# Reordering the front of a fused cross-attention and maxout kernel: state casts, state transposes, the first state read, and idle matmuls at the end

## The chip, the cores and the metric

The kernel runs on one core of a Trainium2 chip. The metric is the device time of one execution in microseconds (us), lower is better. Before the change five runs gave 149.58, 149.90, 149.92, 150.22 and 150.27 us, so the median is 149.92 us.

The engines are named as in the profile: PE is TensorE, DVE is VectorE, ACT is ScalarE, POOL is GpSimd, and SP is the engine whose queue issues nearly all DMA transfers here. PEld is the loading of weights into TensorE.

## What is computed

Eight batches, eight heads, 512 tokens `x` and 32 states `state` of width 64 per head. Tokens read the states and states read the tokens, and the concatenation of both goes through a layer that takes the larger of two products:

```python
scores = scale * x @ state.T            # 512 x 32 for each head
xread  = softmax(scores) @ state        # 512 x 64
scores2 = scale * state @ x.T
sread  = softmax(scores2) @ x           # 32 x 64
t = concat([xread, sread])              # 544 tokens of 8 * 64 = 512
out = maximum(t @ w1, t @ w2) @ w_out   # 512 -> 1024 -> 512
```

Inputs and output are float32; the products run in bfloat16.

## The kernel before

**The algebra.** The maximum is written as relu(t (w1 - w2)) + t w2, so the output is relu(t (w1 - w2)) w_out + t (w2 w_out). `wcat` (128 x 4 x 1536) holds w1 - w2 in its first 1024 columns (`w_sub`, four quarters of 256 columns) and w2 w_out in its last 512 (`w_t` transposes w2, `w_wo` multiplies, `w_wo_out` copies). For each batch the states are multiplied into it once: `u_sw(b, ch)` (L280) makes SW[b] = states x `wcat`, in three chunks `ch` of 512 columns, two of which are for the relu part and the last for the direct one. The attention weights, transposed (`AT[b]`, tile aT), are then multiplied with SW[b] directly, so that xread itself is never formed.

**One batch.** `u_exp` (L216, L219) forms the scores from the transposed tokens `xt` and the block-diagonal states `sbd`, and takes their exponentials `e` on ACT; `u_norm` (L223 to L226) sums, inverts and scales them to `a`; `u_at` or `d_at` transposes `a` into aT; `u_sr` (L239 to L244) makes the state read from `e` and the tokens `xp`, and `u_srt` (L263) transposes it into `sread_t`. `l1` (L308) makes the eight blocks f = 0 to 7 of the hidden layer, each followed by a relu into `r` on ACT and DVE in turn (L296, L298). `l2` has four token groups c: `l2_open` (L319) starts an accumulator with the direct part, `l2_add` (L323) adds `r` times `wo`, `l2_close` copies it out. The state reads of all batches go through the same layer in `moe_sread` near the end.

**PSUM.** Two pools of four banks each turn round: "ps" for everything short, "acc" for the accumulators. A new user of a bank waits until the bank's last reader has finished.

**Where the order comes from.** The schedule is manual: each engine runs its instructions in the order in which the program writes them (L441 to L542). SP likewise issues its transfers in written order, and they share the 16 DMA engines. The order of the loads (L103 to L113) is: states of batch 0, x(0) in two halves, w2 and w_out in pieces, the first 512 columns of w1 in two parts, the second 512 columns of w1, x(1), the states of batches 1 and 2 (`second`), x(2). The rest of the states (`rest`) and x(3) follow later from SP.

**The front, L441 to L530.** It holds, in this order: idle products on a zero tile (`warm_up`, L131); the states of batch 0; tokens of batch 0, cast into `xp` (L180) and transposed on TensorE (L198) into `xt`; scores; w2 cast and transposed while w_out's quarters are cast to `wo` on POOL and multiplied; the first state read; then `u_sw(0, 0)` and `u_sw(0, 2)`, the first half of `l1(0)`, the opens and first adds of `l2(0)` with the states of batches 1 and 2 transposed amid them (L504, L155), `u_sw(0, 1)`, the second half of `l1(0)`, and the preparation of batch 1 between the last adds of batch 0. For batches 1 and 2 the tokens are also cast to a compact copy `xc` (L186), which a DMA transpose (L190) turns into `xt`. From L531 a regular loop takes batches 1 to 7, in which `fillers` puts the next batch's preparation between the products.

Of the kernel before, what the change touches and what calls it, by code (L numbers as in the profile page):

```python
# [15 lines left out]
def kernel(  # L16
# [42 lines left out]
    def copy(eng, o, i):  # L59
        if eng == "A":  # L60
            nc.scalar.copy(o, i)  # L61
        elif eng == "V":
            nc.vector.tensor_copy(o, i)  # L63
        else:
            nc.gpsimd.tensor_copy(o, i)  # L65
# [11 lines left out]
    def load_x(b, parts=1):  # L77
        xf_t[b] = xio.tile([128, H, NC * D], F32, tag="xf", name="xf")
        for g in range(parts):
            nc.sync.dma_start(out=xf_t[b][:, g::parts, :], in_=x[b, g::parts].rearrange("h (p c) d -> p h (c d)", c=NC))  # L80
# [3 lines left out]
    def load_states(bs):  # L84
        nc.sync.dma_start(out=s_f[:, 2 * bs.start:2 * bs.stop],
                          in_=state[bs].rearrange("b (q h) n d -> (h n) (b q) d", q=2))
# [6 lines left out]
    def load_w(t, w, ch, parts=1):  # L93
        cs = slice(ch * 512, (ch + 1) * 512)
        for k in range(parts):
            i = slice(4 * k // parts, 4 * (k + 1) // parts)
            nc.sync.dma_start(out=t[:, i, cs], in_=w.rearrange("(i p) f -> p i f", p=128)[:, i, cs])  # L97
# [9 lines left out]
        load_wo(2 * ch)  # L107
        load_wo(2 * ch + 1)
    load_w(w1f, moe_w1, 0, 2)
    load_w(w1f, moe_w1, 1)  # L110
    load_x(1)
    load_states(second)
    load_x(2)  # L113

    ident = consts.tile([128, 128], BF16)
# [12 lines left out]
    def warm_up(n):  # L128
        p = bank()
        for k in range(n):  # L130
            nc.tensor.matmul(p, warm[:, 0:128], warm, start=(k == 0), stop=(k == n - 1))  # L131


    s_bf = stage.tile([128, 2 * B, 2, D], BF16)
# [25 lines left out]
    def negate_states():  # L160
        for g in range(2):
            gs = slice(64 * g, 64 * g + 64)
            negate("V", sneg[gs], sbd[gs, 0, g::2, g, :])
# [11 lines left out]
    def cast_x(b, parts=(("P", slice(0, 8)),)):  # L175
        new_x(b)
        xp = st[b]["xp"] = xio.tile([128, H, NC, 66], BF16, tag="xp", name="xp")
        nc.gpsimd.memset(xp[:, :, :, 64:65], 1.0)
        for e, hs in parts:
            copy(e, xp[:, hs, :, 0:64], xf_t[b][:, hs].rearrange("p h (c d) -> p h c d", c=NC))  # L180

    def compact_x(b, g, eng="A"):
        new_x(b)
        if g == 0:
            st[b]["xc"] = at.tile([128, H, NC * D], BF16, tag="xc", name="xc")
        copy(eng, st[b]["xc"][:, 4 * g:4 * g + 4], xf_t[b][:, 4 * g:4 * g + 4])  # L186


    def d_xt(b):
# [2 lines left out]
    def u_xt(b, g, eng):  # L192
        d = st[b]
        p = bank(BF16)
        for i in range(4):
            for c in range(NC):
                k = 2 * i + c // 2
                nc.tensor.transpose(p[64 * (c % 2):64 * (c % 2) + 64, k * 128:(k + 1) * 128], d["xp"][:, 2 * i + g, c, 0:64], ident)  # L198
        copy(eng, d["xt"].rearrange("p (i g u) t -> p g i (u t)", g=2, u=2)[:, g], p.rearrange("p (i w) -> p i w", i=4))

    def u_sc(b, g, mul=nc.gpsimd):
# [28 lines left out]
    def u_sr(b):  # L230

        d = st[b]
        d["sr"] = at.tile([128, 2, D], BF16, tag="sr", name="sr")
        d["rr"] = at.tile([128, 2], F32, tag="rr", name="rr")
        p = bank()
        for g in range(2):
            for c in range(NC):
                for i in range(4):
                    nc.tensor.matmul(p[32 * i:32 * i + 32, g * 65:g * 65 + 65], d["e"][:, g, i, c, :],  # L239
                                     d["xp"][:, 2 * i + g, c, 0:65],  # L240
                                     start=(c == 0 and g == 0), stop=(c == NC - 1 and g == 1))
# [146 lines left out]
    def w_cast(o, w, ch, engs="VA"):  # L388
        cs = slice(ch * 512, (ch + 1) * 512)
        for k in range(2):  # L390
            copy(engs[k], o[:, 2 * k:2 * k + 2, cs], w[:, 2 * k:2 * k + 2, cs])
# [26 lines left out]
    def fillers(b):  # L418
        fill = {}

        def put(slot, *units):
            fill.setdefault(slot, []).extend(units)

        n = b + 1
        if n < B:
            put(7, lambda: u_sc(n, 0), lambda: u_sc(n, 1))
            put(8, lambda: u_sr(n))
        if n + 1 < B:
            put(8, lambda: compact_x(n + 1, 0), lambda: compact_x(n + 1, 1))
        if n < B:  # L430
            put(9, lambda: d_at(n))
            put(10, lambda: u_sw(n, 0, 1, 2))
        if n + 1 < B:
            put(10, lambda: d_xt(n + 1))
        if n < B:
            put(11, lambda: u_srt(n))
        return fill

    for b in range(B):
        SW[b] = swt[:, b % 2]  # L440
    warm_up(6)  # L441
    cast_states("V", first)
    states(first)
    warm_up(9)
    cast_x(0, (("A", slice(0, 4, 2)), ("V", slice(4, 8, 2)), ("P", slice(1, 4, 2)), ("V", slice(5, 8, 2))))
    u_xt(0, 0, "V")
    warm_up(2)
    u_xt(0, 1, "A")
    u_exp(0, 0)
    warm_up(2)  # L450
    u_exp(0, 1)
    warm_up(3)
    w_cast(w2b, w2f, 0, "PA")
    u_norm(0, 0, nc.vector)
    u_norm(0, 1, nc.vector)
    w_t(0, 0, "A")
    w_t(0, 1, "A")
    u_sr(0)
    wo_cast(0, "P")
    wo_cast(1, "P")  # L460
    warm_up(1)
    for i in range(4):
        w_wo(0, i)
    u_at(0, "V")
    w_cast(w2b, w2f, 1)
    for i in range(4):
        w_wo(1, i)
    w_t(1, 0, "V")
    w_t(1, 1, "A")
    negate_states()  # L470
    wo_cast(2, "P")
    wo_cast(3, "P")
    u_srt(0)
    warm_up(2)
    for i in range(4):
        w_wo(2, i)
    for e, i in (("P", slice(0, 1)), ("A", slice(1, 2)), ("V", slice(2, 3)), ("A", slice(3, 4))):
# [5 lines left out]
    u_sw(0, 0)  # L483
    u_sw(0, 2)
    w_sub(0)
    w_sub(1)
    l1(0, {}, range(0, 4))
    w_sub(2, nc.vector)
    w_sub(3, nc.vector)
    compact_x(1, 0)  # L490
    compact_x(1, 1)
    d_xt(1)
    load_states(rest)
    cast_x(1, (("A", slice(0, 4)), ("A", slice(4, 8))))
    cast_states("P", second)
    compact_x(2, 0, "P")
    compact_x(2, 1, "P")
    d_xt(2)
    load_x(3)
    for c in range(NC):  # L500
        l2_open(0, c)
    l2_add(0, 0, range(0, 4))
    l2_add(0, 1, range(0, 4))
    states(second)  # L504
    l2_add(0, 2, range(0, 4))
    u_sw(0, 1)
    l2_add(0, 3, range(0, 4))
    l1(0, {}, range(4, 8))
    u_sw(1, 0)
    u_exp(1, 0)  # L510
    u_exp(1, 1)
    u_norm(1, 0, nc.gpsimd)
    u_norm(1, 1, nc.gpsimd)
    cast_states("P", rest)
# [16 lines left out]
    for b in range(1, B):  # L531
        fill = fillers(b)
        if b + 2 < B:
            cast_x(b + 2)
            if b + 3 < B:
                load_x(b + 3)
        if b == 1:
            fill[11].append(lambda: put_states(rest, sT))
        l1(b, fill)
        if b == B - 1:  # L540
            moe_sread()
        l2(b, fill)  # L542


# [28 lines left out]
```

The softmax here doesn't subtract the row's maximum and nothing guards it: scores larger than these inputs give would overflow.

## Time and profile before

| what | value |
|---|---|
| median of the five runs | 149.92 us |
| the profiled execution, its own time | 149.57 us |
| its span, first to last instruction | 147.8 us |
| instructions in it | 3024 |
| PE busy | 141.4 us, 96% |
| DVE, ACT, POOL busy | 81.7, 75.8, 44.2 us |
| granted TensorE clock | 1.000 |
| HBM read and written | 15.20 MB and 8.91 MB |

The page gives each engine's busy time over the whole span and in forty slices. The timeline lists instructions in order of time: start, time taken, engine, line, operation, output and inputs, how many are merged, and in square brackets how long the engine had been idle before and what ended that. The chain of waits goes back from the last instruction through what released each step. PE's busy time includes time in which a product is in the pipe, so neighbouring starts tell more about it than durations do.

### The profile page before, as it was taken

Reading aid. Unit: us, or ns where it says so; the run is one execution under the profiler, and the core shown is the slowest. Engines: PE = TensorE matmul, PEld = TensorE weight load, DVE = VectorE, ACT = ScalarE, POOL = GpSimd, SP = SyncE. Lnnn points to the kernel's source line nnn. Section 1 sums busy time; section 2 is a strip of 40 time slices with the busy share of each in tenths; the row PEclk is TensorE's granted clock in tenths of the full one; section 3 lists DMA queues with packets and bytes.
Section 4 is the critical chain, followed back from the end, with each engine's and each line's share of the span. In section 5 each row is a group of like instructions: output and inputs, shape, how many; then the busy total and the mean of one; then the engine's idle time right before and its main releaser. Section 6 shows DMA issues by size and latency. Waiting matters only on the chain.

```text
span 147.8 us, 3024 instructions
## 1 busy us (share of the span) xinstructions
PE 141.4 (96%) x1249; PEld 67.3 (46%) x1249; DVE 81.7 (55%) x150; ACT 75.8 (51%) x127; POOL 44.2 (30%) x48
## 2 busy tenths in 40 slices
PE   6989899999999999999999999999999999999991
PEld 2445533434454345434443454454445434764460
DVE  5448728758887287545836581667167635721130
ACT  3175548577576268446834691477177036521011
POOL 3145269552957130640072037004100500000000
PEclk9999999999999999999999999999999999999999
DMA  2999999979899969793979497760556031502423
GB/s 72 378 387 386 386 387 342 274 146 218 241 258 330 217 132 304 266 199 125 285 220 174 177 297 175 136 284 2 108 109 284 0 75 64 220 0 71 141 88 133
DMA packets 37982, 29.89 MB, mean 202 GB/s; under 512 B 24912, under 2 KB 33360, under 8 KB 37072
## 3 DMA queue, kind: packets, MB, share of 16 engines
q1 hardware_dynamic: 37824, 29.56, 69.2%
q8 instruction: 10, 0.16, 0.5%
q10 hardware_dynamic: 144, 0.13, 0.3%
q14 instruction: 4, 0.03, 0.1%
HBM read 15.20 MB, written 8.91 MB: 163 GB/s over the span
## 4 chain that ended last, share of the span: by engine, by line
PE 78%; DMA 9%; SPq 9%; POOL 1%; issue 1%; ACT 0%
PE acc L323 35%; PE ps L308 18%; DMA s_f<-in_state_dram 9%; PE acc L319 9%; SPq L97 4%; PE ps L280 3%; SPq L80 3%; PE ps L216 2%; PE ps L367 2%; PE acc L377 2%; SPq L100 2%; PE ps L239 2%; PE acc L357 1%; PE acc L375 1%; PE acc L280 1%; POOL s_bf L65 1%
## 5 line engine op out<-in xcount | busy, mean ns | idle before, releaser
L323 PE MATMUL acc<-wo,r 128*128 128x512 bf16 x248 | 59.0, 379 | 0.0
L323 PEld LDWEIGHTS <-r 128*128 128x128 bf16 x248 | 23.9, 98 | 28.3 <-issue 0.2
L298 DVE TENSOR_SCALAR r<-ps 128x512 bf16<-128x512 f32 x32 | 22.1, 692 | 13.6 <-PE ps L308 13.6
L308 PE MATMUL ps<-aT,swt 128*128 128x512 bf16 x128 | 29.2, 379 | 0.2 <-DVE swt L63 0.2
L226 POOL TENSOR_TENSOR a<-e,er 128x512 bf16<-128x512 bf16 x14 | 14.4, 1048 | 49.1 <-ACT e L219 29.7
L63 DVE COPY ob<-acc 128x512 f32<-128x512 f32 (+1 forms) x17 | 11.1, 655 | 30.2 <-PE acc L323 29.8
L61 ACT COPY ob<-acc 128x512 f32<-128x512 f32 (+1 forms) x16 | 9.2, 574 | 28.8 <-PE acc L323 13.0
L296 ACT ACTIVATE r<-ps 128x512 bf16<-128x512 f32 x32 | 19.3, 602 | 5.7 <-PE ps L308 5.2
L308 PEld LDWEIGHTS <-swt 128*128 128x128 bf16 x128 | 12.0, 98 | 15.0 <-DVE swt L63 0.8
L319 PE MATMUL acc<-swt,aT 128*128 128x512 bf16 x62 | 18.1, 381 | 0.0
L61 ACT CAST swt<-ps 128x512 bf16<-128x512 f32 x18 | 10.0, 589 | 13.0 <-PE ps L280 13.0
L65 POOL CAST xp<-xf 128x2048 bf16<-128x2048 f32 (+1 forms) x7 | 12.2, 1745 | 12.2 <-DMA xf<-in_x_dram 12.2
L61 ACT CAST xc<-xf 128x1024 bf16<-128x1024 f32 x12 | 12.0, 1052 | 1.5 <-DMA xf<-in_x_dram 1.5
L223 DVE TENSOR_REDUCE es<-e 128x16 f32<-128x512 bf16 x16 | 10.6, 660 | 3.6 <-ACT e L219 3.6
L63 DVE CAST swt<-ps 128x512 bf16<-128x512 f32 x18 | 11.6, 679 | 1.1 <-PE ps L280 1.1
L131 PE MATMUL ps<-warm 128*128 128x512 bf16 x25 | 8.0, 447 | 1.3 <-POOL warm L117 1.3
L219 ACT ACTIVATE e<-ps 128x512 bf16<-128x512 f32 x16 | 8.8, 598 | 0.8
L412 PE MATMUL acc<-wo,w2t 128*128 128x512 bf16 x32 | 7.4, 379 | 0.6 <-POOL wo L65 0.6
L319 PEld LDWEIGHTS <-aT 128*128 128x128 bf16 x62 | 4.7, 98 | 6.0 <-issue 2.5
L280 PE MATMUL ps<-wcat,sbd 64*32 64x512 bf16 x136 | 6.2, 383 | 0.1
L216 PEld LDWEIGHTS <-xt 128*128 128x128 bf16 x128 | 4.8, 98 | 2.8 <-ACT xt L61 0.8
L65 POOL CAST wo<-wof 128x1024 bf16<-128x1024 f32 x4 | 4.3, 1064 | 5.1 <-DMA wof<-in_moe_w_out_dram 5.1
(74 smaller groups left out, 119.4 us busy)
## 6 DMA issues: line engine op xcount, KB each, us to landing
xf<-in_x_dram SPq DMA_DIRECT2D x7, 1024.0 KB, 7.6
out_dram<-ob SPq DMA_DIRECT2D x7, 1024.0 KB, 5.0
w2f<-in_moe_w_dram SPq DMA_DIRECT2D x2, 1024.0 KB, 9.0
wof<-in_moe_w_out_dram SPq DMA_DIRECT2D x4, 512.0 KB, 10.9
xf<-in_x_dram SPq DMA_DIRECT2D x2, 512.0 KB, 4.4
w1f<-in_moe_w_dram SPq DMA_DIRECT2D x2, 512.0 KB, 13.3
w1f<-in_moe_w_dram SPq DMA_DIRECT2D x1, 1024.0 KB, 14.1
out_dram<-ob SPq DMA_DIRECT2D x3, 256.0 KB, 2.6
```

Source lines behind the costliest of these rows:

```text
L61: nc.scalar.copy(o, i)
L63: nc.vector.tensor_copy(o, i)
L65: nc.gpsimd.tensor_copy(o, i)
L219: nc.scalar.activation(out=d["e"][:, g].rearrange("p i c n -> p (i c n)"), in_=p, func=ACTF.Exp, scale=scale)
L223: nc.vector.tensor_reduce(d["es"][:, g], d["e"][:, g].rearrange("p i c n -> p (i c) n"), axis=mybir.AxisListType.X, op=ALU.add)
L226: mul.tensor_mul(d["a"][:, g].rearrange("p c i n -> p i c n"), d["e"][:, g], d["er"][:, g].rearrange("p (i c) -> p i c", i=4).unsqueeze(3) ...
L280: nc.tensor.matmul(pg[g][32 * i:32 * i + 32, :], sneg[gs, i, :] if k else sbd[gs, b, 2 * i + g, g, :], w[gs, i, ch * 512:(ch + 1) * 512], ...
L296: nc.scalar.activation(out=o, in_=p, func=ACTF.Relu)
L298: nc.vector.tensor_scalar(o, p, scalar1=0.0, scalar2=None, op0=ALU.max)
L308: nc.tensor.matmul(p, SW[b][:, g, f * 128:(f + 1) * 128], AT[b][:, g, :], start=(g == 0), stop=(g == 1))
L319: nc.tensor.matmul(OB[b][1 + c], AT[b][:, g, c * 128:(c + 1) * 128], SW[b][:, g, FF:WC], start=(g == 0), stop=False)
L323: nc.tensor.matmul(OB[b][1 + c], R[b][:, f, c * 128:(c + 1) * 128], wo[:, f, :], start=False, stop=(f == NF - 1))
```

## The change

In the loads, the second 512 columns of w1 move behind x(1) and the states of batches 1 and 2. At the start six idle products become three, and four later groups go or shrink (two, two, three and one become one; two more go further on). Batch 0's tokens are first cast to the compact `xc`, from which TensorE transposes 128 x 128 blocks, and cast to `xp` later, on ACT. The negated states are made earlier on DVE. The second half of w2's first cast is DVE's instead of ACT's, the second w2 cast goes ahead of aT, and the second w2 transposes stand between the products of w_out's second quarter.

Further on, the state read `u_sr(0)` goes behind the first half of `l1(0)` and its transpose `u_srt(0)` behind the second half. The states of batches 1 and 2 are cast on POOL between the two subtractions `w_sub(0)` and `w_sub(1)`, and transposed between the second and the third open of `l2(0)`. `w_sub(2)` and `w_sub(3)` come later on DVE. The scores of batch 1 move into the second half of `l1(0)`, behind block f = 5. At the very end TensorE gets 26 products of 8 x 8 on the zero tile.

```diff
     load_w(w1f, moe_w1, 0, 2)
-    load_w(w1f, moe_w1, 1)
     load_x(1)
     load_states(second)
+    load_w(w1f, moe_w1, 1)
     load_x(2)
...
+    def pad_stream(n):
+        p = bank()
+        for k in range(n):
+            nc.tensor.matmul(p[0:8, 0:8], warm[:, 0:8], warm[:, 0:8], start=(k == 0), stop=(k == n - 1))
...
-            for c in range(NC):
-                k = 2 * i + c // 2
-                nc.tensor.transpose(p[64 * (c % 2):64 * (c % 2) + 64, k * 128:(k + 1) * 128], d["xp"][:, 2 * i + g, c, 0:64], ident)
+            for cp in range(2):
+                k = 2 * i + cp
+                nc.tensor.transpose(p[:, k * 128:(k + 1) * 128], d["xc"][:, 2 * i + g, cp * 128:(cp + 1) * 128], ident)
...
-    warm_up(6)
+    warm_up(3)
     cast_states("V", first)
     states(first)
     warm_up(9)
-    cast_x(0, (("A", slice(0, 4, 2)), ("V", slice(4, 8, 2)), ("P", slice(1, 4, 2)), ("V", slice(5, 8, 2))))
+    negate_states()
+    compact_x(0, (("A", slice(0, 4, 2)), ("V", slice(4, 8, 2)), ("P", slice(1, 4, 2)), ("V", slice(5, 8, 2))))
     u_xt(0, 0, "V")
-    warm_up(2)
     u_xt(0, 1, "A")
     u_exp(0, 0)
-    warm_up(2)
     u_exp(0, 1)
-    warm_up(3)
-    w_cast(w2b, w2f, 0, "PA")
+    warm_up(1)
+    w_cast(w2b, w2f, 0, "PV")
     u_norm(0, 0, nc.vector)
     u_norm(0, 1, nc.vector)
     w_t(0, 0, "A")
     w_t(0, 1, "A")
-    u_sr(0)
     wo_cast(0, "P")
     wo_cast(1, "P")
-    warm_up(1)
     for i in range(4):
         w_wo(0, i)
+    w_cast(w2b, w2f, 1)
     u_at(0, "V")
-    w_cast(w2b, w2f, 1)
-    for i in range(4):
-        w_wo(1, i)
+    w_wo(1, 0)
+    w_wo(1, 1)
     w_t(1, 0, "V")
     w_t(1, 1, "A")
-    negate_states()
+    w_wo(1, 2)
+    w_wo(1, 3)
+    cast_x(0, (("A", slice(0, 4)),))
+    copy("A", st[0]["xp"][:, 4:8, :, 0:64], xf_t[0][:, 4:8].rearrange("p h (c d) -> p h c d", c=NC))
     wo_cast(2, "P")
     wo_cast(3, "P")
-    u_srt(0)
-    warm_up(2)
...
     w_sub(0)
+    cast_states("P", second)
     w_sub(1)
     l1(0, {}, range(0, 4))
-    w_sub(2, nc.vector)
-    w_sub(3, nc.vector)
-    compact_x(1, 0)
-    compact_x(1, 1)
+    u_sr(0)
+    compact_x(1)
     d_xt(1)
     load_states(rest)
     cast_x(1, (("A", slice(0, 4)), ("A", slice(4, 8))))
-    cast_states("P", second)
-    compact_x(2, 0, "P")
-    compact_x(2, 1, "P")
+    l2_open(0, 0)
+    l2_open(0, 1)
+    states(second)
+    l2_open(0, 2)
+    l2_open(0, 3)
+    w_sub(2, nc.vector)
+    w_sub(3, nc.vector)
+    l2_add(0, 0, range(0, 4))
+    l2_add(0, 1, range(0, 4))
+    compact_x(2, (("P", slice(0, 4)), ("P", slice(4, 8))))
     d_xt(2)
     load_x(3)
-    for c in range(NC):
-        l2_open(0, c)
-    l2_add(0, 0, range(0, 4))
-    l2_add(0, 1, range(0, 4))
-    states(second)
     l2_add(0, 2, range(0, 4))
     u_sw(0, 1)
     l2_add(0, 3, range(0, 4))
-    l1(0, {}, range(4, 8))
     u_sw(1, 0)
-    u_exp(1, 0)
-    u_exp(1, 1)
+    l1(0, {5: [lambda: u_exp(1, 0), lambda: u_exp(1, 1)]}, range(4, 8))
+    u_srt(0)
     u_norm(1, 0, nc.gpsimd)
     u_norm(1, 1, nc.gpsimd)
...
         l2(b, fill)
+    pad_stream(26)
```

`compact_x` now takes a list of engines and head ranges, as `cast_x` did; what it does for batches 1 to 7 stays as it was.

More of the change, by code (lines that the diff above doesn't have):

```diff
@@ L180, in cast_x, with compact_x @@
             copy(e, xp[:, hs, :, 0:64], xf_t[b][:, hs].rearrange("p h (c d) -> p h c d", c=NC))
-    def compact_x(b, g, eng="A"):
+    def compact_x(b, parts=(("A", slice(0, 4)), ("A", slice(4, 8)))):
         new_x(b)
-        if g == 0:
-            st[b]["xc"] = at.tile([128, H, NC * D], BF16, tag="xc", name="xc")
-        copy(eng, st[b]["xc"][:, 4 * g:4 * g + 4], xf_t[b][:, 4 * g:4 * g + 4])
+        xc = st[b]["xc"] = at.tile([128, H, NC * D], BF16, tag="xc", name="xc")
+        for e, hs in parts:
+            copy(e, xc[:, hs], xf_t[b][:, hs])
     def d_xt(b):
@@ L428, in fillers @@
         if n + 1 < B:
-            put(8, lambda: compact_x(n + 1, 0), lambda: compact_x(n + 1, 1))
+            put(8, lambda: compact_x(n + 1))
         if n < B:
```

## The prediction

> **What bounds the kernel now.** I read the page first, by its 40 slices, to see where TensorE waits and for whom.
>
> ```profile
> PE   6989899999999999999999999999999999999991
> ...
> GB/s 72 378 387 386 386 387 342 274 146 218 241 258 330 217 132 304 266 199 125 285 220 174 177 297 175 136 284 2 108 109 284 0 75 64 220 0 71 141 88 133
> ...
> PE 78%; DMA 9%; SPq 9%; POOL 1%; issue 1%; ACT 0%
> ```
>
> One slice is 3.7 us. TensorE has gaps only in the first six; there the transfers run at a level 386 GB/s. From 26 us on TensorE is full. The chain of waits shows the seam:
>
> ```profile
> 14.48 13.45 DMA s_f<-in_state_dram
> 27.93 0.05 issue
> 27.98 1.15 POOL s_bf L65
> 29.14 0.05 issue
> 29.18 0.40 PE ps L155 x4
> ```
>
> After 29.18 it holds TensorE pieces alone up to 144.59. But the states, late as they are, cost little: the previous group, 8 products (L323) from 27.23 at 0.216 each (the steady starts: 16 in 3.45), ends at 28.96, so the wait is 0.22. What starts the full stretch lies earlier. The timeline from 21 to 24.5 us:
>
> ```profile
> 21.48 0.43 DVE L63 CAST w1b<-w1f 128x512 bf16<-128x512 f32 x1 [2.66 <-DMA w1f<-in_moe_w_dram]
> ...
> 21.83 1.28 DVE L63 CAST wcat<-acc 128x512 bf16<-128x512 f32 x2
> ...
> 23.03 1.28 DVE L63 CAST swt<-ps 128x512 bf16<-128x512 f32 x2
> ...
> 23.76 1.04 PE L308 MATMUL ps<-aT,swt 128*128 128x512 bf16 x4 [0.21 <-DVE swt L63]
> ```
>
> VectorE idles 2.66 us for the second half of w1's first 512 columns, then runs four copies, and the first l1 product starts at 23.76. TensorE arrives at the same point by its own road: wo's third quarter lands at 17.5, its cast ends at 18.57, 16 products (L412) fill 18.62 to 22.07. So **the start of l1(0) at 23.76 is set by transfers; from there TensorE sets the time.** l1(1) starts at 39.85, and batches 1 to 7, whose order of instructions is unchanged, follow without a gap. The whole question: does 23.76 move, and does the stretch of 16.09 us from there to 39.85 get longer or shorter?
>
> **Before 23.76: nothing.** Removed are 12 of 25 idle products (0.427 apart at first, 0.216 later), 16 transposes (32 of 64x128, 0.64 per 16, become 16 of 128x128; 0.5 per 8 by the w2b transposes, L401, 16 in 1.06; 0.32 by 0.040 each if width were free), u_sr(0) (0.37) and u_srt(0) (0.06). All of it lies beside transfers: the w2b transposes wait at 10.53 for the POOL cast of w2f, the products at 18.62 for wo. The transfers up to w1's first half keep their place on SP, so 17.5 and 21.43 stand. The ScalarE copies of xp(0), 2 x 1.04, moved behind the w2t copy (ends 18.58), end by 20.7; the first w1b cast slips from 20.13 to 20.7 and ends at 21.3, still ahead of the 21.48 one. The copies hold the x buffer for load_x(2), issued at 20.64 anyway. On VectorE the w2b cast (0.68) goes ahead of the softmax sums (es 9.88 to 10.1); the second w2b cast goes ahead of aT, 14.95 to 15.6; aT is wanted at 23.76. The negation (1.09) fits ahead of x's second half (6.70). Cover gone, these would cost at most their durations, one for one.
>
> The row for the clock: idle products start 0.43 apart up to 3.4 us and the 16 at 18.62 run at 0.216, right behind the longest idle of TensorE, 0.61 us; that gap grows to some 1.1 us (17.5 to 18.6). [...]
>
> **The stretch from 23.76, in the new order** (listed from the changed program; durations from the chain of waits: 2 products 0.43, 8 are 1.73; state-weight products with their hand-over 0.44; scores 0.47; u_sr 0.37).
>
> 25.50 u_sr(0), 25.87 two opens, 26.73 state transposes (0.24), 26.97 two opens, 27.83 three adds, 30.52 u_sw(0,1), 30.86 add, 31.82 u_sw(1,0), 32.16 l1 f4 and f5, 33.02 scores of batch 1, then f6, f7, u_srt(0), add. Who must be ready:
>
> - *States.* Loads issued on SP behind w1's first half were w1's second half, x(1), states, x(2), landing at about 24.3, 27.41, 27.93, 31.04. Now x(1) takes the first place (24.3), the states 24.8 (0.52 behind x(1), as before), and w1's second half, last of the same three, 27.9. SP issues the same list inside 10.19 to 20.46, x(2) still behind. On POOL: subtraction 0 ends at 24.0, cast 1.15 to 26.0, TensorE wants it at 26.73: the wait of 0.22 goes. Subtraction 1 ends at 28.5 (before 26.44); u_sw(1,0) wants it at 31.82.
> - *w1's second half.* VectorE: f3 to 26.39, state-read normalisation 0.46, sbd copies 27.16 to 28.02, subtractions 2 and 3 (2.35) to 30.39, wanted at 30.52. It just fits; before it had 1.7 us to spare (28.66 against 30.38). This is late next: each us of landing after 28.0 is a us lost.
> - *x(1).* ScalarE compacts at 25.87 instead of 27.41, so the DMA transpose is issued at 27.98 instead of 29.43; 4.4 to landing gives 32.4. Scores want it at 33.0. The old wait for xt, 0.11, goes.
> - *Banks.* The old second group of scores waited 0.16 (0.63 against 0.47) for VectorE's f7. Now the first waits about 0.05 for its swt copy (to 33.01).
> - *ScalarE.* Here is the new wait. In these rows of before
>
> ```profile
> 33.13 0.60 ACT L296 ACTIVATE r<-ps 128x512 bf16<-128x512 f32 x1 [0.27 <-PE ps L308]
> ...
> 33.90 0.68 PEld L216 LDWEIGHTS <-xt 128*128 128x128 bf16 x16 [0.33 <-DMA xt<-xc]
> 33.90 0.80 PE L216 MATMUL ps<-sbd,xt 128*128 128x64 bf16 x16
> ...
> 34.44 1.10 ACT L219 ACTIVATE e<-ps 128x512 bf16<-128x512 f32 x2
> ...
> 34.53 1.03 PE L323 MATMUL acc<-wo,r 128*128 128x512 bf16 x4
> ```
>
> f6's relu (33.13) is done before the exponentials, and the adds start at once. In the new order the scores stand between f5 and f6, so f6's relu queues behind two exponentials: scores at 33.07, exponentials 0.54 later, 33.61 to 34.71, relu f6 to 35.31. TensorE has done f6, f7, u_srt by 34.46, adds f4 and f5 by 34.89, and waits for f6 until 35.37: 0.48. Behind it on ScalarE stand sread_t and the swt copies, whose readers come later.
>
> After that: u_sw(1,1) at 35.90 against 35.49. POOL's weights a(1) end at about 38.6 (before 38.26), wanted at 38.8, so nothing more is added and l1(1) starts at 40.26.
>
> **Sum.** Moved in +0.43; waits gone -0.49 (0.22, 0.11, 0.16); new waits +0.53 (0.05, 0.48); shorter hand-overs in my list -0.06: **+0.41 us**.
>
> *The pad.* 26 pairs of 8-column products are not in the trace: 0.029 each by the 64-column scores, 0.06 by the state transposes, so 0.75 to 1.6 us from 144.6. The last copy and store run there until 147.8, 3.2 us: zero; with no cover, up to 1.6. A gain is excluded: nothing follows them.
>
> The profiled execution took 149.57 (span 147.8 and 1.77 around it), the lower end of the runs, whose median is 149.92. 149.57 + 0.41 = 149.98; on the median's footing **150.3**.
>
> **Rivals.**
>
> 1. *Not slower: ScalarE clears in time.* If f6's relu starts by 34.2 instead of 34.7, both new waits vanish and -0.12 is left: **149.8**. For it: the relu is ready at 34.25 by TensorE. Against: every step in front has a row of 0.55 to 0.60, none shorter.
> 2. *A transfer is late.* The transpose of x(1) now starts with x(2) still in flight. xt landed after 4.4 at best, but 6.0 and 6.6 in other batches: landing 34.0 to 34.6 costs 0.9 to 1.5. w1's second half late by 0.3 to 1 costs the same. **151.0**, up to 151.8.
> 3. *l1(0) starts earlier.* If w1's first half lands sooner, since x(1) follows it in the queue, each 0.1 counts fully; 0.5 us or more from the front makes it faster, to about **149.4** and below. Against: level 386 GB/s, same bytes ahead.
> 4. *The clock falls* in the thinner front: 16 products at 0.427 end at 25.4 instead of 22.07, **153**.
>
> **Numbers.** Forecast 52%, spread 0.2 each way (its waits are differences of some 0.5). Half of that lies within 0.3% (0.45 us, about what a measurement of this kernel tells from none), half above. Rival 1 18% (5 of it faster), rival 2 18%, rival 3 8%, rival 4 4%. So faster 0.13, within 0.38, slower 0.49. Range 149.4 to 151.8: rival 1's low side and rival 2's bound; without rival 4 and most of rival 3.
>
> **What would show it.** First l1 product at 23.8; state transposes at 26.7 without a wait; idle of the adds before batch 0's f6, put down to ScalarE's relu, of 0.4 to 0.5; subtraction 3 ending within 0.3 of u_sw(0,1); l1(1) at 40.2 to 40.3; pad over before the last store lands. Wrong if 23.76 moves, or xt or the subtraction is what the stretch waits for.

## The result, and the profile after

The changed kernel has a median of 150.31 us (44 runs, 149.65 to 151.47) against 149.78 us of the kernel before (79 runs, 149.50 to 151.28): a ratio of 1.0040, with a 95% interval of 1.0029 to 1.0052. It is slower by half a microsecond, more than the 0.3% that this kernel's measurement can tell from no change. One run each of the kernels a2_no_pad and d1_rest_behind_xt2 below was in a slower state (152.62 and 153.00 us) and stands in no median, ratio or count here.

The profiled execution of the changed kernel took 149.65 us with a span of 147.9 us, and so stands at the low end of its own runs. It is read first for the order, and the sum is made later on a repeat of the same kernel (a0_control, 149.98 us) that lies nearer its median. From L138 on, lines of the changed kernel are numbered 7 higher than in the kernel before.

The page of the changed kernel, TensorE's 40 slices, instruction fetches, and the chain's shares by engine:

```profile
PE   5956999999999999999999999999999999999993
...
q8 instruction: 9, 0.15, 0.4%
...
PE 78%; SPq 11%; DMA 7%; DVE 2%; issue 1%
```

TensorE reads 9 from the fifth slice on, and the last slice reads 3 instead of 1: those are the 26 small products. The row of instruction fetches counts 9 in the span where the page before has 10; that will matter. The chain no longer has POOL in it. Its seam has moved, as the chain of waits of the changed kernel shows:

```profile
17.24 10.64 DMA w1f<-in_moe_w_dram
27.88 0.02 issue
27.90 2.47 DVE wcat L393 x2
30.37 0.04 issue
30.42 0.41 PE ps L287 x8
```

Before, the states' transfer and cast stood here. Now it is the second half of w1, then VectorE's subtractions 2 and 3 (L393), then `u_sw(0, 1)`: what the forecast named as late next, with 0.13 us to spare. The timeline of the changed kernel, start, time taken, engine, line, operation, and in brackets the idle time before and what ended it:

```profile
20.92 0.43 DVE L63 CAST w1b<-w1f 128x512 bf16<-128x512 f32 x1 [3.05 <-DMA w1f<-in_moe_w_dram]
...
23.29 1.90 PE L315 MATMUL ps<-aT,swt 128*128 128x512 bf16 x8 [0.21 <-DVE swt L63]
...
30.42 0.41 PE L287 MATMUL ps<-wcat,sbd 64*32 64x512 bf16 x8 [0.21 <-DVE wcat L393]
```

In this execution the first half of w1 landed early, and the first l1 product stands at 23.29 instead of 23.76. Part of the 0.47 is given back at 30.42: the 12 adds ahead of it, 0.216 each from 27.45, end at 30.04, and the next product starts 0.38 later, where the control below takes 0.09. The bracket puts 0.21 of this down to the subtraction. The first l1 product of batch 1 comes at 39.95, against 39.85 before.

The table has this for every profile of the study: S0 is the first l1 product, "stretch" runs from S0 to the first l1 product of batch 1, "rest" from there to the end of the span, and "xt" gives when the DMA transpose of x(1) was issued and how long it took to land.

| kernel | S0 | stretch | rest | span | its own us | xt issued, landing |
|---|---|---|---|---|---|---|
| before | 23.76 | 16.09 | 107.95 | 147.8 | 149.57 | 29.43, 4.4 |
| after | 23.29 | 16.66 | 107.95 | 147.9 | 149.65 | 27.30, 5.2 |
| a0_control (after again) | 23.91 | 16.38 | 107.91 | 148.2 | 149.98 | 27.92, 4.6 |
| a1_warmups_back | 23.85 | 16.38 | 109.07 | 149.3 | 151.12 | 27.86, 4.6 |
| a2_no_pad | 23.92 | 17.34 | 107.94 | 149.2 | 150.98 | 27.93, 6.3 |
| a3_scores_behind_f7 | 23.89 | 16.07 | 107.94 | 147.9 | 149.68 | 27.90, 4.6 |
| c0_scores_no_pad | 23.98 | 16.18 | 107.94 | 148.1 | 149.87 | 27.99, 6.3 |
| c1_state_read_in_front | 24.03 | 16.18 | 107.89 | 148.1 | 149.92 | 28.04, 6.3 |
| c2_before_state_read_late | 23.89 | 16.52 | 107.89 | 148.3 | 150.11 | 29.44, 4.5 |
| c3_before_with_pad | 23.76 | 16.07 | 107.97 | 147.8 | 149.54 | 29.29, 4.5 |
| d1_rest_behind_xt2 | 24.14 | 16.37 | 107.89 | 148.4 | 150.21 | 28.14, 4.4 |
| e1_c1_rest_moved | 24.03 | 16.09 | 107.98 | 148.1 | 149.84 | 28.04, 6.2 |
| e2_e1_split_subtraction | 24.01 | 16.32 | 107.97 | 148.3 | 150.04 | 28.02, 4.6 |
| g1_before_states_early | 23.72 | 16.54 | 107.94 | 148.2 | 149.96 | 29.96, 4.5 |

Control against before: S0 +0.15, stretch +0.29, rest -0.04, span +0.40. So nothing that the change did reaches beyond batch 0, with one exception at the very end that only the scatter shows.

### The profile page after: what moved, and what is told of

The parts are those of the page before. It is cut to its first block, busy times and chain, and to the rows that moved or that the text cites. A ratio compares the mean times of both kernels' runs of the same rounds, so it can differ in the third digit from the quotient of the medians.

```text
span 147.9 us, 3024 instructions
## 1 busy us (share of the span) xinstructions
PE 140.2 (95%) x1247; PEld 67.4 (46%) x1247; DVE 82.0 (55%) x151; ACT 76.6 (52%) x128; POOL 44.3 (30%) x48
## 4 chain that ended last, share of the span: by engine, by line
PE 78%; SPq 11%; DMA 7%; DVE 2%; issue 1%
PE acc L330 35%; PE ps L315 18%; PE acc L326 9%; DMA w1f<-in_moe_w_dram 7%; SPq L85 4%; SPq L97 3%; PE ps L287 3%; PE ps L374 2%; PE acc L384 2%; SPq L100 2%; PE ps L223 2%; PE ps L246 2%; DVE wcat L393 2%; SPq L80 1%; PE acc L364 1%; PE acc L382 1%
## 5 line engine op out<-in xcount | busy, mean ns | idle before, releaser
L330 PE MATMUL acc<-wo,r 128*128 128x512 bf16 x248 | 59.0, 379 | 0.0
L330 PEld LDWEIGHTS <-r 128*128 128x128 bf16 x248 | 24.0, 98 | 29.1 <-ACT r L303 0.5
L315 PEld LDWEIGHTS <-swt 128*128 128x128 bf16 x128 | 11.9, 98 | 14.7 <-DVE swt L63 0.5
L61 ACT CAST xc<-xf 128x1024 bf16<-128x1024 f32 (+1 forms) x13 | 12.6, 1019 | 3.9 <-DMA xf<-in_x_dram 3.9
L65 POOL CAST xp<-xf 128x2048 bf16<-128x2048 f32 x6 | 11.3, 1891 | 9.7 <-DMA xf<-in_x_dram 9.7
L63 DVE CAST swt<-ps 128x512 bf16<-128x512 f32 x18 | 11.7, 680 | 1.9 <-PE ps L287 1.9
L419 PE MATMUL acc<-wo,w2t 128*128 128x512 bf16 x32 | 7.5, 380 | 0.7 <-ACT w2t L61 0.7
L131 PE MATMUL ps<-warm 128*128 128x512 bf16 x13 | 5.9, 612 | 1.3 <-POOL warm L117 1.3
L287 PE MATMUL ps<-wcat,sbd 64*32 64x512 bf16 x136 | 6.2, 382 | 0.2 <-DVE wcat L393 0.2
L223 PE MATMUL ps<-sbd,xt 128*128 128x64 bf16 x128 | 5.2, 193 | 0.9 <-ACT xt L61 0.9
```

The costliest lines, as they stand in the source:

```text
L223: nc.tensor.matmul(p[:, k * 64:k * 64 + 64], d["xt"][:, 4 * i + 2 * g + cp, :], sbd[:, b, 2 * i + g].rearrange("p u n -> p (u n)"), start= ...
L287: nc.tensor.matmul(pg[g][32 * i:32 * i + 32, :], sneg[gs, i, :] if k else sbd[gs, b, 2 * i + g, g, :], w[gs, i, ch * 512:(ch + 1) * 512], ...
L315: nc.tensor.matmul(p, SW[b][:, g, f * 128:(f + 1) * 128], AT[b][:, g, :], start=(g == 0), stop=(g == 1))
L330: nc.tensor.matmul(OB[b][1 + c], R[b][:, f, c * 128:(c + 1) * 128], wo[:, f, :], start=False, stop=(f == NF - 1))
```

## The experiments

The theory was the forecast's: the scores of batch 1 between f5 and f6 make f6's relu queue behind two exponentials on ScalarE, and the moved state read costs what the vanished waits gain. The rivals: the thinner front (fewer idle products) lets l1 start later; the transfer of xt is late; something at the tail, where the stream of TensorE now ends otherwise, costs time.

Each kernel was timed in five rounds beside runs of the kernel before on the same chip. Ratios are to those, with their 95% interval.

| kernel | median us (runs) | before beside it | ratio |
|---|---|---|---|
| a0_control | 150.16 (12) | 149.73 | 1.0041 [1.0013, 1.0068] |
| a1_warmups_back | 151.08 (9) | 149.73 | 1.0085 [1.0059, 1.0112] |
| a2_no_pad | 150.13 (11) | 149.73 | 1.0023 [0.9997, 1.0049] |
| a3_scores_behind_f7 | 149.93 (12) | 149.73 | 1.0010 [0.9986, 1.0034] |
| c0_scores_no_pad | 149.84 (12) | 149.72 | 1.0005 [0.9986, 1.0025] |
| c1_state_read_in_front | 149.89 (12) | 149.72 | 1.0018 [1.0003, 1.0034] |
| c2_before_state_read_late | 150.18 (6) | 149.72 | 1.0038 [1.0024, 1.0052] |
| c3_before_with_pad | 149.76 (12) | 149.72 | 1.0002 [0.9986, 1.0018] |
| d1_rest_behind_xt2 | 150.13 (11) | 149.73 | 1.0031 [1.0013, 1.0048] |
| e1_c1_rest_moved | 149.84 (11) | 149.73 | 1.0003 [0.9993, 1.0013] |
| e2_e1_split_subtraction | 150.13 (12) | 149.73 | 1.0024 [1.0014, 1.0035] |
| g1_before_states_early | 150.09 (11) | 149.74 | 1.0024 [1.0015, 1.0033] |

### The changed kernel again

> The changed kernel itself, as a control beside the next three. Queue theory (the stretch from the first l1 product to l1(1) grew from 16.1 us by 0.4 to 0.6, since batch 0's f6 waits about 0.5 for the relu behind two exponentials, and u_sr and u_srt add 0.43, against 0.49 of waits gone): about 150.3, first l1 product of a typical profile near 23.8. Thin-front theory (fewer idle products leave TensorE slow or late in the front): about 150.3 too, but the first l1 product of a typical profile later than 23.9, and the stretch not longer than 16.3.

No edit. 150.16 us; the profile has the ScalarE wait where it was forecast. The timeline of a0_control from 33 to 36 us:

```profile
33.29 0.63 PE L223 MATMUL ps<-sbd,xt 128*128 128x64 bf16 x16
33.72 1.08 ACT L226 ACTIVATE e<-ps 128x512 bf16<-128x512 f32 x2
...
34.69 0.60 ACT L303 ACTIVATE r<-ps 128x512 bf16<-128x512 f32 x1
34.72 1.28 PE L330 MATMUL acc<-wo,r 128*128 128x512 bf16 x4
35.34 0.10 PEld L330 LDWEIGHTS <-r 128*128 128x128 bf16 x1 [0.53 <-ACT r L303]
```

The adds (L330) start at 34.72, do f4 and f5, and then TensorE's weight load waits for ScalarE's `r`, the relu of f6 that began only at 34.69, right behind the exponentials. Four products take 1.28 instead of the 1.03 that they take where nothing is waited for: the wait costs 0.25. The stretch is 0.29 longer than before, less than the 0.4 to 0.6 expected, and S0, at 23.91, lies just where the two theories part, so this run alone does not decide between them.

One row of this page differs from the pages of before and after, which read 9 in all slices. It is the TensorE clock that was granted, in tenths, in the page of a0_control:

```profile
PEclk9995999999999999999999999999999999999999
```

In finer stretches it is 1.00 up to 11.6 us, 0.50 from 11.8 to 15.0 and 1.00 again from 15.2 on.

### The idle products put back

> The changed kernel with all 25 idle products of before back in their places. Queue theory: within 0.15 of the control, about 150.3, stretch 16.5 to 16.7 as in the control. Thin-front theory: 0.3 to 0.5 below the control, 149.8 to 150.0, with the first l1 product earlier by as much.

```diff
-    warm_up(3)
+    warm_up(6)
+    warm_up(2)    # and (2), (3) for (1), (1), (2) further on, in the old places
```

S0 23.85 and stretch 16.38 are those of the control to 0.06, where the theory of the thinner front wanted S0 earlier by 0.3 to 0.5. In these two profiles taking the idle products out did not start l1 later. Both wait for w1: VectorE's first cast of its second part starts at 21.57 here and at 21.64 in the control, and S0 follows 2.28 and 2.27 later (before: 21.48, and 2.28).

But the two differ in the clock. In the control's stretch of half clock (0.50) the products stand 0.43 apart instead of 0.216. The timeline of TensorE in a0_control:

```profile
11.06 1.31 PE L408 MATMUL ps<-ident,w2b 128*128 128x128 bf16 x16 [1.06 <-POOL w2b L65]
...
13.62 2.22 PE L419 MATMUL acc<-wo,w2t 128*128 128x512 bf16 x6 [0.22 <-issue]
...
22.28 0.41 PE L287 MATMUL ps<-w1b,sbd 64*32 64x512 bf16 x8
```

The same in a3_scores_behind_f7, whose order up to here is the control's and whose clock stayed at 1.00:

```profile
11.24 1.07 PE L408 MATMUL ps<-ident,w2b 128*128 128x128 bf16 x16 [1.06 <-POOL w2b L65]
...
21.37 0.40 PE L287 MATMUL ps<-w1b,sbd 64*32 64x512 bf16 x4
```

From the w2 transposes (L408) to the first product of `u_sw` (L287) TensorE takes 11.22 us in the control and 10.13 in a3. The control hides the 1.09, since w1 comes no earlier; c0 does not, as the account of S0 below shows. How often the clock falls is seen in each run's mean granted clock, 0.988 in the control's profile: 18 of the 56 runs of the changed kernel (with the control) have 0.986 to 0.989, none of the 9 runs of a1 has less than 0.992, and none of 105 of the kernel before less than 0.995. So the clock falls in about one run of three of the changed kernel. That the idle products had kept it up fits these counts, but nine runs are few. The median span is 148.3 us for the 18 runs and for the other 38 alike.

Yet a1 is slower than the control by 0.9 us, all of it behind the last product. The transfers of a1_warmups_back in the last 7 us, KB and median us from issue to landing:

```profile
q8 instruction: 1, 0.02, 1.6%
...
out_dram<-ob SPq DMA_DIRECT2D x1, 256.0 KB, 4.3
out_dram<-ob SPq DMA_DIRECT2D x1, 128.0 KB, 3.8
out_dram<-ob ACTq DMA_DIRECT2D x1, 128.0 KB, 3.1
```

The same view of a0_control, which has no such row of queue q8:

```profile
out_dram<-ob SPq DMA_DIRECT2D x1, 256.0 KB, 2.0
out_dram<-ob SPq DMA_DIRECT2D x1, 128.0 KB, 1.9
out_dram<-ob ACTq DMA_DIRECT2D x1, 128.0 KB, 1.9
```

With the idle products back, the tenth fetch of instructions, 16 KB, falls at 144.4 us, among the last three stores; they land 1.2 to 2.3 us later. In the kernel before, whose tenth fetch is at 141.8, the same stores take 2.6, 2.1 and 1.9. The control has no fetch behind 128.7.

### The pad taken out

> The changed kernel without the 26 small products at the end. Prediction: within 0.15 of the control, since they are over 2 us before the last store has landed. If the pad costs time against that: 0.2 or more below the control.

```diff
-    pad_stream(26)
```

The median, 150.13 us, is within 0.15 of the control, as expected. Its profile met something else. The timeline of a2_no_pad:

```profile
34.29 0.64 PE L223 MATMUL ps<-sbd,xt 128*128 128x64 bf16 x16 [0.84 <-DMA xt<-xc]
...
36.36 0.10 PEld L330 LDWEIGHTS <-r 128*128 128x128 bf16 x1 [0.57 <-ACT r L303]
```

The DMA transpose of x(1), issued at 27.93 as in the control, landed after 6.3 us instead of 4.6. TensorE waited 0.84 for it and then, as before, for ScalarE: stretch 17.34, 0.96 more than the control. This is the forecast's second rival, at its price of 0.9 to 1.5, in a kernel whose front is the control's.

What the pad does shows in the time outside the span: in the 11 runs of a2_no_pad it is never above 1.83 us. In the 56 runs of the changed kernel (with the control) it is 2.0 or more in 14, up to 2.97; in 105 runs of the kernel before, never above 1.95. So with the pad in this order the kernel loses up to 1.2 us behind the span, in one run of four.

### The scores of batch 1 behind f7

> The changed kernel with the scores of batch 1 behind block f7 of l1(0) instead of behind f5. Queue theory: the wait for f6's relu goes, about 0.4 to 0.5 below the control, 149.8 to 149.9, stretch about 16.1 to 16.2. Thin-front theory: within 0.15 of the control.

```diff
-    l1(0, {5: [lambda: u_exp(1, 0), lambda: u_exp(1, 1)]}, range(4, 8))
+    l1(0, {}, range(4, 8))
+    u_exp(1, 0)
+    u_exp(1, 1)
```

The timeline of a3_scores_behind_f7:

```profile
33.89 0.60 ACT L303 ACTIVATE r<-ps 128x512 bf16<-128x512 f32 x1 [0.26 <-PE ps L315]
34.12 0.63 PE L223 MATMUL ps<-sbd,xt 128*128 128x64 bf16 x16
34.56 1.09 ACT L226 ACTIVATE e<-ps 128x512 bf16<-128x512 f32 x2
...
34.65 1.03 PE L330 MATMUL acc<-wo,r 128*128 128x512 bf16 x4
```

f6's relu runs at 33.89, ahead of the exponentials, and the four adds take 1.03 without a wait. The stretch is 16.07, 0.31 shorter than the control's. 149.93 us: by the medians this one order makes up for about half of the loss of the control, and its ratio to before no longer differs from 1. The pad is still in, and 4 of its 12 runs end 2.0 us or more outside the span.

### Both undone: scores behind f7, no pad

> The changed kernel with the scores of batch 1 behind block f7 and without the pad. In the control and in the run with the scores behind f7, some executions lie 0.6 to 0.9 further outside the span than the usual 1.75 to 1.9; without the pad none did. Fetch theory (with the pad TensorE's stream of 2496 rows just reaches one more fetch of instructions, behind its end, which some executions wait for): the time outside the span is 1.7 to 1.95 in every run, median 149.8. Rival (that scatter is of the chip): some runs at 2.3 to 2.7 outside the span, median as with the pad, 149.9. By both the stretch from the first l1 product to l1(1) is 16.0 to 16.2.

Edits of a2 and a3 together. 149.84 us, 1.0005 [0.9986, 1.0025], and 1.82 at most outside the span. Nothing is left of the loss in the median, and all else that the change does gains nothing there. Its two shortest spans, 147.4 at a granted clock of 1.000, do lie below the shortest of the 105 runs of before, 147.6. xt landed after 6.3 us here too, but with the scores behind f7 that is seen only by 0.11 in the stretch (16.18 against 16.07).

### The state read back in the front

> The run before, and the state read of batch 0 taken out of the stretch: between w_out's third and fourth quarter, with half of xp's cast on VectorE, which is idle there. Queue theory: TensorE had 0.3 to 0.6 us to spare for w1 before the first l1 product, so that product stays at 23.9 and 0.37 leaves the stretch (15.7 to 15.8): 149.4 to 149.5, 0.2 to 0.3 below the kernel before. Rival (the front is as full as the stretch): the first l1 product moves to 24.2 and nothing is gained, 149.8.

```diff
-    copy("A", st[0]["xp"][:, 4:8, :, 0:64], xf_t[0][:, 4:8]...)
+    copy("V", st[0]["xp"][:, 4:8, :, 0:64], xf_t[0][:, 4:8]...)
...
     w_wo(2, i)
+    u_sr(0)
...
     l1(0, {}, range(0, 4))
-    u_sr(0)
```

On top of c0. If the state read's half microsecond was what the waits gained had to pay, this should have been ahead of before. It is not: 149.89. S0 is not the reason: at 24.03 it stands 2.28 behind the cast of w1 (21.75), where w1 sets it. Three rows say why, the timeline of c1_state_read_in_front:

```profile
30.59 0.41 PE L287 MATMUL ps<-wcat,sbd 64*32 64x512 bf16 x8
...
34.36 0.52 PEld L223 LDWEIGHTS <-xt 128*128 128x128 bf16 x16 [0.71 <-DMA xt<-xc]
34.36 0.64 PE L223 MATMUL ps<-sbd,xt 128*128 128x64 bf16 x16 [0.22 <-ACT r L303]
```

TensorE comes to `u_sw(0, 1)` earlier, at about 30.31 by the lengths of what stands ahead of it, but the subtraction lets it go at 30.59; and xt, landing 6.3 after 28.04, holds the weight load of the scores until 34.36. In this profile, what is taken off TensorE in the stretch becomes a wait for w1's second half and for xt.

### In the kernel before, only the state read moved

> The kernel before with one part of the change alone: u_sr(0) behind the first half of l1(0), u_srt(0) behind the second. Queue theory: 0.43 more in the stretch, less the 0.22 that TensorE waited for the states there, so +0.2: 149.9 to 150.0. Rival (the front gains as much as the stretch loses): no change, 149.7.

```diff
     w_t(0, 1, "A")
-    u_sr(0)
...
     l1(0, {}, range(0, 4))
+    u_sr(0)
...
-    u_srt(0)
...
     l1(0, {}, range(4, 8))
+    u_srt(0)
```

Stretch +0.43, more than the 0.2 expected, since the wait for the states was to vanish and did not. The timeline of c2_before_state_read_late:

```profile
26.83 2.35 DVE L386 TENSOR_TENSOR wcat<-w1f,w2f 128x1024 bf16<-128x1024 f32 x2
...
27.98 1.67 POOL L65 CAST s_bf<-s_f 128x512 bf16<-128x512 f32 x1 [1.25 <-DMA s_f<-in_state_dram]
...
29.71 0.40 PE L155 MATMUL ps<-ident,s_bf 128*128 128x128 bf16 x4
```

The states' cast on POOL took 1.67 where it takes 0.61 in the control, and the transposes came 0.5 later than before. VectorE's subtractions had slipped by 0.5 (0.13 of it with S0) behind the state read's normalisation and end at 29.18; the cast ends 0.47 after them. The last section comes back to this.

### In the kernel before, only the pad added

> The kernel before with the 26 small products at its end, 2552 rows. Fetch theory: its tenth fetch lies at 141.8, ahead of the last stores, and the pad reaches no further one: within 0.15 of before, nothing beyond 2.0 outside the span. Rival (the small products themselves cost): 0.2 or more above before, with runs at 2.3 to 2.9 outside the span.

Edit: `pad_stream(26)` at the end of before. 149.76, 1.0002 [0.9986, 1.0018], no run above 1.82 outside the span. Here the tenth fetch comes at 141.6, ahead of the last stores. So the pad's products as such cost nothing, as forecast, and what goes with it in the changed kernel needs this order too. That the place of the next fetch decides it fits (148.5 in after, behind the span), but is not shown.

### The remaining states behind the next transpose

> The changed kernel with one load moved: the last states (rest, 320 KB in small pieces) are issued behind the DMA transpose of x(2) instead of right behind that of x(1). In the profiles of the changed order so far the transpose of x(1) landed 4.6 to 5.2 us after its issue, or 6.3, and the 6.3 made scores wait 0.8. Theory A (the small pieces of rest, issued 0.1 behind it, get between its last pieces): it lands 4.4 to 5.2 after its issue in the profile, and no run has a span of 149.0 or more; median 150.0, fewer slow ones than the control's 2 in 12. Theory B (x(2), still in flight when it is issued, is what delays it): 6.3 and spans of 149.2 stay.

```diff
     d_xt(1)
-    load_states(rest)
...
     d_xt(2)
+    load_states(rest)
```

Whether the many small pieces of `load_states(rest)`, issued right behind the transpose of x(1), delay it. In the profile xt landed after 4.4, but 2 of 11 runs still have spans of 149.1 and 149.3, as 11 of 56 of the changed kernel have 149.0 or more, and 2 of 105 of before. 150.13 us, as the control. So neither theory is decided here.

### The same on c1

> The run with the state read in the front, scores behind f7 and no pad, and the load of rest behind the transpose of x(2). There the transpose of x(1) landed 6.3 after its issue and held the scores until 34.36, which ate what the state read had freed. Theory A: it lands by 32.6 to 33.2, the scores start at 34.0, stretch 15.8 to 15.9, median 149.5. Theory B: as that run, stretch 16.2, 149.9.

xt landed after 6.2 with the small pieces out of the way. The late landing does not need them; that theory falls. 149.84 us.

### The last subtraction shared with POOL

> The run before, with a quarter of the last subtractions (128 of 512 columns) on POOL, which is idle there, and the rest in one piece on VectorE. In the run with the state read in front u_sw(0,1) started 0.2 to 0.3 after TensorE was ready. Queue theory: that goes, another 0.2 below the run before: stretch 15.6, 149.3. Rival (two engines on the same data slow each other, or x(1)'s transpose still sets the scores): same as the run before.

```diff
-    w_sub(2, nc.vector)
-    w_sub(3, nc.vector)
+    for eng, cs in ((nc.vector, slice(512, 896)), (nc.gpsimd, slice(896, 1024))):
+        eng.tensor_sub(wcat[:, :, cs], w1f[:, :, cs], w2f[:, :, cs])
```

Meant to bring `u_sw(0, 1)` forward on top of e1. The timeline of e2_e1_split_subtraction:

```profile
28.07 1.86 DVE L504 TENSOR_TENSOR wcat<-w1f,w2f 128x1536 bf16<-128x1536 f32 x1 [0.18 <-DMA w1f<-in_moe_w_dram]
28.33 2.72 POOL L504 TENSOR_TENSOR wcat<-w1f,w2f 128x512 bf16<-128x512 f32 x1
31.10 0.41 PE L287 MATMUL ps<-wcat,sbd 64*32 64x512 bf16 x8 [0.65 <-POOL wcat L504]
```

POOL's quarter took 2.72, though a piece of twice the width takes 2.36 there (at 25.95 in this profile) while VectorE does not subtract. It ended 1.12 after VectorE's part, and TensorE waited 0.65 for it. 150.13, slower than e1 by 0.3.

### In the kernel before, the states loaded and cast early

> The kernel before, with what the changed one does for the states at no cost: the states of batches 1 and 2 (128 KB) are loaded ahead of x(1) but behind all of w1, and cast on POOL right behind the second subtraction; and x(1) is compacted by ScalarE and POOL together (half each) instead of ScalarE alone. Queue theory: the wait of 0.22 for the states goes, the DMA transpose of x(1) is issued at about 28.9 instead of 29.43, lands 4.4 to 4.6 later at 33.4, so the 0.11 before the scores goes too: stretch from the first l1 product to l1(1) 15.75 to 15.9, median 149.4 to 149.5. Theory B (a transpose issued while x(2) is in flight can land 6.2 to 6.3 later): issued at 28.9, just when x(2)'s data end, it is late in some or all runs, scores wait until 35.1, and the median is 149.7 or more with runs near 150.5.

```diff
-    load_x(1)
     load_states(second)
+    load_x(1)
...
     w_sub(1)
+    cast_states("P", second)
...
-    compact_x(1, 1)
+    compact_x(1, 1, "P")
```

The part of the change that did work, the earlier states, put into before without the rest; it was also to issue the transpose earlier, at 28.9. The timeline of g1_before_states_early:

```profile
26.27 2.76 DVE L386 TENSOR_TENSOR wcat<-w1f,w2f 128x1024 bf16<-128x1024 f32 x2
26.34 1.62 POOL L65 CAST s_bf<-s_f 128x512 bf16<-128x512 f32 x1
27.90 2.03 POOL L65 CAST xc<-xf 128x1024 bf16<-128x1024 f32 x1
28.91 0.39 PE L155 MATMUL ps<-ident,s_bf 128*128 128x128 bf16 x4
...
34.46 0.64 PE L216 MATMUL ps<-sbd,xt 128*128 128x64 bf16 x16 [0.91 <-DMA xt<-xc]
```

The wait for the states is gone (28.91, without a bracket). But both casts on POOL meet VectorE's subtractions, the tokens' cast takes 2.03 instead of 1.04, the transpose is issued at 29.96 instead of 29.43, and the scores wait 0.91 for it. 150.09 us. A wait of 0.22 was traded for one of 0.91. As the issue came late, this run does not tell whether x(2) in flight makes the transpose late.

No version was ahead of the kernel before; the intervals of a2, a3, c0, c3 and e1 include no difference from it.

## Why the prediction was right, and where its terms were off

The forecast was +0.41 on the profiled execution and 150.3 on the median's footing; measured were 150.31 and, between the profiles of control and before, +0.40. The mechanism held, the new wait on ScalarE above all, but the agreement of the total is partly luck: between the profiles the stretch grew by 0.29, not 0.41, and S0 by 0.15, not 0.

- *"Before 23.76: nothing."* In the control S0 is later by 0.15, and this is w1: VectorE's first cast behind it stands at 21.64 instead of 21.48. But the forecast took the transfers alone, and TensorE's own road is about as long. In the ten profiles of the changed order that cast starts at 20.53 to 20.92 in three (after, c0, d1) and at 21.57 to 21.75 in seven. Where w1 is late, S0 stands 2.28 behind the cast; where it is early, S0 stands 1.45 behind the first product of `u_sw`, which follows TensorE's products of w2 and w_out (L419): 23.29 in after, and 23.98 and 24.14 in c0 and d1, whose granted clock was 0.50 for some 3.4 us from about 11.9 on, as in the control. The timeline of c0_scores_no_pad:

```profile
20.53 0.43 DVE L63 CAST w1b<-w1f 128x512 bf16<-128x512 f32 x1 [1.97 <-DMA w1f<-in_moe_w_dram]
...
21.77 0.69 DVE L63 CAST wcat<-acc 128x512 bf16<-128x512 f32 x1 [0.81 <-PE acc L419]
...
22.53 0.41 PE L287 MATMUL ps<-w1b,sbd 64*32 64x512 bf16 x8
...
23.98 0.61 PE L315 MATMUL ps<-aT,swt 128*128 128x512 bf16 x2 [0.21 <-DVE swt L63]
```

  w1 is cast at 20.53, and VectorE then waits for TensorE's products (L419), behind which the first product of `u_sw` starts at 22.53. At full clock, 10.13 behind the w2 transposes at 11.31, it would have started at 21.44 and S0 would have come at about 22.9, an estimate. So the half clock cost c0 about 1.1, and the control nothing.
- *State read moved in, +0.43.* Measured 0.54: `u_sr(0)` takes 0.48 with the gap of 0.11 in front of it, between products of 128x128 tiles and its own of 128x32 (25.64, the end of eight l1 products at 0.216, over its start at 25.75, to 26.12 in the control; 25.62 to 26.09 in c2), and `u_srt(0)` 0.06. I had left out the gap, about 0.1.
- *Waits gone, -0.49.* All three gone in the control: the states are cast at 25.27, between the two POOL subtractions, and transposed at 26.99 without a wait. The timeline of a0_control:

```profile
25.27 0.61 POOL L65 CAST s_bf<-s_f 128x512 bf16<-128x512 f32 x1 [1.00 <-DMA s_f<-in_state_dram]
...
25.75 0.44 PE L246 MATMUL ps<-xp,e 128*32 128x65 bf16 x32
26.99 0.39 PE L162 MATMUL ps<-ident,s_bf 128*128 128x128 bf16 x4
```

- *The new ScalarE wait, +0.48.* The mechanism is shown: the releaser in a0, and its absence in a3. Its size was 0.25, half the forecast. I took the two exponentials as 1.10, a merged row's whole length; the next relu starts 0.97 after the first of them (33.72 to 34.69), since in these rows the instructions on ScalarE overlap at their ends: 0.60 long, but 0.49 from start to start. The rest is that TensorE itself came to the adds about 0.1 later behind S0 than forecast, by the gap before `u_sr(0)`. The wait for a bank was about 0.02 instead of 0.05.
- *w1's second half "just fits".* Shown at its limit: it costs 0.2 to 0.3 in the profile of after, where S0 is early, and in c1. The forecast named a stretch that waits for the subtraction as a sign of being wrong; in the control it does not wait. So rival 3, an earlier l1(0), did happen in after, and gave about half of what its price said: S0 is 0.62 earlier than in the control, the first l1 product of batch 1 only 0.34, since this wait took the rest.
- *Rival 2, the late transpose.* Real in a share of runs. xt landed after 6.2 or 6.3 in 4 of the 10 profiles of the changed order, and after 4.4 or 4.5 in all four of before's order, where it is issued at 29.29 or later. With the scores behind f5 that costs 0.96 (a2). By the spans of 149.0 and more, 11 of 56 runs of the changed kernel met it, if all these are of this cause, which no profile of them shows. The cause isn't settled: the small pieces are not needed for it (e1), and x(2), still in flight when the transpose is issued at 28 and landed by 31, fits but was not tried by itself.
- *Rival 1, ScalarE in time:* refuted by a0. *Rival 4, the clock:* it did fall, in about one run of three (18 of 56), but earlier than the rival had it and at a smaller price. The products that it priced still came 0.216 apart (20 from 17.43 in after); those between 12.8 and 15.1 in the control did not, and cost from 0 to 1.1 (a0, c0). That the sum has nothing for the clock was my estimate; no run shows what makes it fall, and TensorE's longest idle since its first product was 1.06 to 1.12 us where it fell (a0, c0, d1) and 1.05 to 1.06 where it did not (after, a2, a3).
- *The pad, zero.* Right inside the span: the 26 products run from 144.60 to 145.39, under the last copy and store. What I did not consider is the time outside it (2.0 us or more in 14 of 56 runs; without the pad, in none of the 11 of a2). A gain was excluded, and none came.

The means of the runs show how much of the agreement is luck. The 56 runs of the changed kernel take 150.45 us on average, the 105 of before 149.80, which is +0.65: 0.47 in the span and 0.18 outside it. Without the 11 spans of 149.0 and more the span's share is 0.26. So in its usual runs the new order costs less than the forecast's 0.41, and long spans and late ends, which the sum had at zero, bring the total to where the forecast had it. (The forecast's chances, added up from their own parts, are 0.39 within and 0.48 slower, not 0.38 and 0.49.)

So the order of the change removes three waits of 0.49 in sum, pays them back with the state read (0.54), and adds a wait on ScalarE (0.25). The 0.15 in front is the landing of w1 in that profile.

## What to carry to other kernels

When a piece that has a producer and a consumer is put between two other such pairs, look at the in-order queue of the engine between them: the relu that TensorE wants next stood behind two exponentials that it wanted much later, and moving these by two blocks won the time back (0.31 of the stretch, a0 to a3). Take queue times from start to start of neighbours (here 0.49 for each exponential), not from the length of a merged row (1.08 for two). Measure the scatter, of the span and of what lies outside it, where a change moves a transfer or the length of an instruction stream: one profile showed neither the late transpose (6.3 us in a2, 5.2 in after) nor the late end (up to 2.97 us outside the span in other runs). And read the granted clock slice by slice: a mean of 0.988 looks like nothing, and was 3.4 us at half clock.

## What the runs showed of the hardware

**Beside VectorE's subtraction POOL's instructions ended late.** Where VectorE subtracts two float32 inputs meanwhile, the ends of POOL's cast or subtraction fit waiting, not running slowly. Ends of VectorE's subtraction and of the POOL instruction that was issued beside it: c2, 29.18 and 29.65; before, 28.66 and 29.12; e2, 29.93 and 31.05. From the first to the second is 0.47, 0.46 and 1.12, against 0.61, 0.61 and about 1.18 (half of 2.36) for the same POOL instruction where VectorE does not subtract. In g1 it goes both ways: VectorE's two subtractions also take 2.76 instead of 2.35. By this reading the forecast's 1.15 for the states' cast was 0.61 and a wait; why the two engines wait for each other is not shown.

**Beside a fetch of instructions the last stores landed late.** With 16 KB on queue q8 at 144.4 us the last three stores landed 3.1 to 4.3 us after issue instead of 1.9 to 2.0, and the span was 1.1 us longer (a1). That the fetch is the cause is read from the two standing together; no run moved the fetch alone. The profile of the changed kernel has a tenth fetch at 148.5, just behind the end of its span, while the control's and a3's have none. The late ends outside the span belong to this order with the pad (after, its control, a3, and one run of 2.07 in d1); none of the kernels without the pad (a2, c0, c1, e1, e2) had one. That such a fetch is their cause fits, but was not shown. A fetch did not always show as lost time: TensorE is not idle at the eight fetches from 40.9 to 141.8 us in the profile of before, nor at the seven from 48.4 to 128.3 in that of after.

**The granted clock was halved in three profiles, behind idle times of TensorE hardly longer than elsewhere.** In a0, c0 and d1 it was 0.50 for some 3.4 us (11.7 to 15.1 in a0), and products stood 0.43 apart instead of 0.216. TensorE's longest idle ahead of it was 1.06 to 1.12 us; in after, a2 and a3, of the same order, it was 1.05 to 1.06, and the clock stayed at 1.00 there. So the longest gap does not tell which run is hit; what does is open.

**The DMA transpose of x(1) landed at one of two times**, 4.4 to 5.2 or 6.2 to 6.3 us after issue in the 14 profiles, with the same bytes each time.
